# Linear attention's denominators gathered into one PSUM bank per superblock

## The chip, the cores and the metric

One core of one Trainium2 chip. The metric is device microseconds (us) of one execution: the kernel before has a median of 287.94 us over 3 runs (287.43 to 290.42). The profiled execution took 287.51 us, of which 285.5 us are its span from the first to the last instruction.

## The reference

Two attention blocks, A and B, run on inputs of their own (2048 tokens, width 640, 32 heads of 20), and their outputs stand side by side. A is a softmax with a sliding window of 256 tokens. B is linear attention, and the change is in B alone:

```python
def _B_ref(x, wqkv, wo):
    ...
    phi = lambda t: jnp.where(t > 0, t + 1, jnp.exp(t)) + 1e-6
    pq, pk = phi(q), phi(k)
    kv = jnp.einsum("bhsd,bhse->bhde", pk, v)
    z = jnp.einsum("bhsd->bhd", pk)
    num = jnp.einsum("bhqd,bhde->bhqe", pq, kv)
    den = jnp.einsum("bhqd,bhd->bhq", pq, z)[..., None] + 1e-6
    o = num / den
    return (lambda x, *d: x.transpose(*d))(o, 0, 2, 1, 3).reshape(B, S, D) @ wo
```

## The kernel before

The 2048 tokens are four superblocks of 512 (`SB`), each of four token blocks of 128 (`TPS`); the width of 640 is five chunks of 128 (`KT`). The main loop is written out by hand and goes through 90 **units** of A. A unit multiplies queries with keys into the four-bank tile `S_ps` on TensorE (PE), takes the exponential `p<-S_ps` on ScalarE (ACT), masks it on GpSimd (POOL), and two units later multiplies the result with the values into `O_ps` (PE, 16 short matmuls of 21 columns), which VectorE (DVE) divides into `otokA` (`recA`, then `otokA`). `S_ps` has one buffer, so the score matmuls of a unit start only when the exponential of the unit before has ended.

Everything else is **fill**: generators that yield how many matmul columns they have issued, and from which `take` pulls after each unit. The constants `EARLY`, `FILL` and `TAIL` fix how many columns are taken: (352320 - 17920 - 2 * 1024) / 90, about 3692 columns a unit. What the fill still has after the last unit is issued at once, and then comes `a_out_last`, the output projection of A's last superblock, which needs the transposes `oT<-otokA` that SP (SyncE) issues after the last `O_ps`.

Fill of block B that matters here:

- `b_q(s)` projects the queries of superblock s, one bank for each of the five chunks. `phi` takes the exponential on ACT at once (`e<-dense`), but its two DVE operations (`rest`: `e<-e`, then `phi<-dense,e`) are put into the list `later`. `flush()` records them behind the next evacuation or the next `phi`.
- `b_num(s)` makes numerators and denominators together. `kv_bd` holds for each head 20 columns of k-v sums and, as column 21 (`HV` = `DH` + 1), the sum of phi(k); heads that a chunk doesn't own are zero. For each of 4 token blocks and 2 halves of 16 heads, 3 matmuls (147, 147 and 84 columns) fill one bank, and DVE does `denB<-dense` (an add of 1e-6), `denB<-denB` (the reciprocal) and `otokB<-dense,denB` (the multiplication). Half 0 reads the chunks 0 to 2 of phi(q), half 1 the chunks 2 to 4. After each token block SP issues one transpose `xA<-otokB`.
- `outs` are the output projections, in the order `a_out(0)`, `b_out(0)`, ... `b_out(2)`, each of five banks: four of 5 matmuls of 512 columns and one of 20 matmuls of 128. `early` are A's projections for its last superblock.
- `even(a, na, b, nb, lead)` mixes banks of two generators; with `lead=True` a bank of `b` comes first.

All these banks come from the pool `dense` (`dps`), which has 3 buffers. A fourth bank can be filled only when the evacuation of the first is done. PE, DVE, ACT, POOL and SP each run their own instructions strictly in the order in which the program recorded them.

Of the kernel before, what the change touches and what calls it, by code (L numbers as in the profile page):

```python
# [9 lines left out]
P = 128  # L10
# [3 lines left out]
BF16 = mybir.dt.bfloat16  # L14
F32 = mybir.dt.float32

H = 32
DH = 20
HV = DH + 1
NG = H // 4  # L20
SB = 512
TPS = SB // P
# [32 lines left out]
def kernel(  # L55
# [10 lines left out]
    nc = tc.nc  # L66
    _, S, D = A_x.shape
    KT = D // P
# [8 lines left out]
    def pool(name, bufs, space=None):  # L77
        if space is None:
            return ctx.enter_context(tc.tile_pool(name=name, bufs=bufs))
        return ctx.enter_context(tc.tile_pool(name=name, bufs=bufs, space=space))  # L80
# [11 lines left out]
    rp = pool("rows", 4)  # L92
    op = pool("o", 2)
    sp = pool("small", 4)
    sps = pool("sps", 1, PSUM)
    ops = pool("ops", 1, PSUM)
    dps = pool("dps", 3, PSUM)
# [55 lines left out]
    heads_of = []  # L153
# [24 lines left out]
    def flush():  # L178

        while later:  # L180
            later.pop(0)()
# [8 lines left out]
    def bank():  # L190
        return dps.tile([P, SB], F32, name="dense")
# [9 lines left out]

    def phi(dst, src, view=lambda t: t[:]):

        e = sp.tile([P, SB], BF16, name="e")
        nc.scalar.activation(out=view(e), in_=src, func=ACT.Exp)  # L205
        flush()

        def rest():
            nc.vector.tensor_scalar(  # L209
                out=e[:], in0=e[:], scalar1=1e-6, scalar2=1.0 + 1e-6, op0=ALU.add, op1=ALU.min  # L210
            )
            nc.vector.scalar_tensor_tensor(  # L212
                out=dst, in0=src, scalar=0.0, in1=view(e), op0=ALU.max, op1=ALU.add
            )

        later.append(rest)
# [4 lines left out]
    def even(a, na, b, nb, lead=False):  # L221


        def one(g):
            for c in g:
                yield c
                if isinstance(c, End):
                    break

        done = 0  # L230
        for i in range(na):
            while lead and done < nb and done * na <= i * nb:
                done += 1
                yield from one(b)
            yield from one(a)
            while not lead and done * na < (i + 1) * nb:
                done += 1
                yield from one(b)
        yield from a


    xA, xB = {}, {}
# [18 lines left out]
    def a_qk(s, between=()):  # L261
        for n, base in (("q", 0), ("k", D)):
            st = stp.tile([P, KT, SB], BF16, name="st")
            for c in range(KT):
                ps = bank()
                yield from chain(
                    ps[:],
                    lambda kt: w_sb["A"][:, kt, base + c * P : base + (c + 1) * P],
                    lambda kt: xA[s][:, kt, :],
                    SB,  # L270
                )
                evac(st[:, c, :], ps[:])
                if c == KT - 1:
                    pad, pl, name = (q_pad, qp, "qpad") if n == "q" else (k_pad, kp, "kpad")
                    pad[s] = pl.tile([P, NG, SB], BF16, name=name)
                    if n == "q":
                        q_reads = bounce(n, s, st, pad[s])
                        for g in between:
                            yield from g
                    else:  # L280
                        late_reads[s] = bounce(n, s, st, pad[s])
                        q_reads()
                yield End(SB)
# [30 lines left out]
    def a_v(s):  # L314
        v_tok[s] = v_bufs[s % 3]
        yield from v_proj("A", xA[s], v_tok[s])
# [42 lines left out]
    kv_bd = wp.tile([P, KT, NHC, HV], BF16, name="kv_bd")  # L359

    def b_kv(s):
        pk = pqp.tile([P, TPS, D], BF16, name="phi")

        def done(tb, ps):
            if tb is None:
                phi(pk[:, :, SB:D], ps, lambda t: t[:].rearrange("p (t n) -> p t n", n=P))
            else:
                phi(pk[:, tb, 0:SB], ps[:])

        rows = tok_rows(xB[s], w_sb["B"], D, done)  # L370
        values_of = v_proj("B", xB[s], vB)
        yield from even(rows, TPS + 1, values_of, TPS + 1)
        yield from values_of
        flush()
# [22 lines left out]
    hh = H // 2  # L397
    half_parts = []
    for i in range(2):
        parts = []  # L400
        for c in range(KT):
            a, b = heads_of[c]
# [5 lines left out]
    oT_B = {}  # L408

    pq_of = {}  # L410

    def b_q(s):
        xt = xB[NS + s]
        pq = pqp.tile([P, KT, SB], BF16, name="phi")
        pq_of[s] = pq
        for c in range(KT):
            ps = bank()
            yield from chain(
                ps[:],
                lambda kt: w_sb["B"][:, kt, c * P : (c + 1) * P],  # L420
                lambda kt: xt[:, kt, :],
                SB,
            )
            phi(pq[:, c, :], ps[:])
            if s == 0:
                keep_own_head(kv_bd, c)
            yield End(SB)

    def b_num(s):
        flush()  # L430
        pq = pq_of[s]
        oT_B[s] = xp.tile([P, KT, SB], BF16, name="xA")
        for tb in range(TPS):
            ot = rp.tile([P, D], BF16, name="otokB")
            for i in range(2):
                ps = bank()
                ov = ps[:, 0 : hh * HV].rearrange("p (h e) -> p h e", e=HV)
                parts = half_parts[i]
                for n, (c, ho, nh, col) in enumerate(parts):
                    nc.tensor.matmul(  # L440
                        ov[:, col : col + nh, :],
                        lhsT=pq[:, c, tb * P : (tb + 1) * P],
                        rhs=kv_bd[:, c, ho : ho + nh, :],
                        start=(n == 0),
                        stop=(n == len(parts) - 1),
                        skip_group_check=True,
                    )
                den = sp.tile([P, hh, 1], F32, name="denB")
                nc.vector.tensor_scalar_add(
                    out=den[:], in0=ov[:, :, DH:HV], scalar1=1e-6  # L450
                )
                nc.vector.reciprocal(out=den[:], in_=den[:])
                nc.vector.tensor_tensor(  # L453
                    out=ot[:, i * hh * DH : (i + 1) * hh * DH].rearrange(
                        "p (h e) -> p h e", e=DH
                    ),
                    in0=ov[:, :, 0:DH],
                    in1=den[:].to_broadcast([P, hh, DH]),
                    op=ALU.mult,
                )  # L460
                flush()
                yield End(3 * 150)
            nc.sync.dma_start_transpose(
                out=oT_B[s][:, :, tb * P : (tb + 1) * P], in_=ot[:]
            )

    def b_out(s):
        yield from wo_proj("B", oT_B[s], s, D)
# [102 lines left out]
    def a_out(s):  # L571
        yield from wo_proj("A", oT_A[s], s, 0)
# [22 lines left out]
    def load(n, s):  # L595
        if n == "A":
            xA[s] = load_x("A", s)
        else:
            xB[s] = load_x("B", s % NS)
        yield 0  # L600

    def seq(*gens):
        for g in gens:
            yield from g
# [27 lines left out]
    def k_reads(s, gen):  # L632
        return hook(gen, 8, lambda: late_reads[s]())

    early = seq(a_v(3), a_qk(3))
    outs = seq(a_out(0), b_out(0), a_out(1), b_out(1), a_out(2), b_out(2))
# [13 lines left out]
        b_kv(3),  # L650
        load("B", NS + 1),
        even(b_q(0), KT, early, 2),
        load("B", NS + 2),
        even(b_num(0), 2 * TPS, early, 2 * TPS, lead=True),
        early,
        k_reads(3, b_q(1)),
        load("B", NS + 3),
        even(b_num(1), 2 * TPS, outs, 2 * TPS, lead=True),
        even(b_q(2), KT, outs, 2),
        even(b_num(2), 2 * TPS, outs, 2 * TPS, lead=True),  # L660
        even(b_q(3), KT, outs, 2),
        even(b_num(3), 2 * TPS, outs, 2 * TPS, lead=True),
        outs,
        b_out(3),
    )
# [16 lines left out]
    for i, (okey, first, last, parts) in enumerate(units):  # L682
        p = scores(okey[0], parts)
# [44 lines left out]
```

## Time and profile before

| | |
|---|---|
| median of 3 runs | 287.94 us |
| profiled execution: its time, its span | 287.51 us, 285.5 us |
| busy: PE, DVE, ACT, POOL | 271.2, 181.4, 199.5, 159.5 us |
| granted TensorE clock | 0.999 |
| `kv_bd` matmuls of `b_num` (L440) | 96 |
| `denB<-dense` (L449), `denB<-denB` (L452), `otokB` (L453) | 32 each; mean 164, 253, 492 ns |
| first and last of the L440 matmuls | 157.9 and 267.4 us |

Busy time of an engine is the time in which one of its recorded instructions ran. Matmuls overlap one another, so a duration of one (173 ns for 21 columns) says little of how fast a row of them is issued. In a line of the timeline stand start and duration in us, engine, line of the kernel, operation, output<-input, and how many; in square brackets how long the engine was idle before it and for whom it waited. ACT's exponential `p<-S_ps` marks the units: the time from the start of one to the start of the next is the length of a unit.

### The profile page before, as it was taken

The numbers are of one execution on the slowest core, as the hardware profiler recorded it, in microseconds if no ns is written. First come the engines' busy times: TensorE is split into PE (matmuls) and PEld (weight loads), VectorE is DVE, ScalarE is ACT, GpSimd is POOL, SyncE is SP. The second block draws the span as 40 slices with busy tenths as digits, with TensorE's granted clock in tenths as the row PEclk, the third lists the DMA queues.
The fourth block names the chain that finished last, engine by engine and source line by source line (L and its number), as shares of the span: only waits on it lengthen the run. The fifth ranks groups of instructions, "written<-read, shape, count | busy, mean of one in ns | idle before, by whom it ended". The sixth has DMA issues, their size and how long they took to land.

```text
span 285.5 us, 8251 instructions
## 1 busy us (share of the span) xinstructions
PE 271.2 (95%) x3512; PEld 156.7 (55%) x3512; DVE 181.4 (64%) x409; ACT 199.5 (70%) x227; POOL 159.5 (56%) x205
## 2 busy tenths in 40 slices
PE   7999999898999999999998799998999989999995
PEld 7644555564655754555654464444655555546652
DVE  0666657549656745547656785468866886678861
ACT  2000069968979888889889588897889868978402
POOL 4000036656656666666678666665766776676620
PEclk9999999999999999999999999999999999999999
DMA  7997699989152762273053522179865228022566
GB/s 247 296 316 217 165 206 178 109 162 270 32 117 47 146 88 94 72 144 63 3 117 72 115 49 77 40 171 125 148 137 72 79 61 141 3 78 64 136 172 200
DMA packets 68116, 35.91 MB, mean 126 GB/s; under 512 B 50800, under 2 KB 67184, under 8 KB 68080
## 3 DMA queue, kind: packets, MB, share of 16 engines
q1 hardware_dynamic: 65760, 29.50, 51.7%
q0 software_dynamic: 1008, 4.59, 4.7%
q10 hardware_dynamic: 1312, 1.31, 1.5%
q8 instruction: 27, 0.44, 0.7%
q14 instruction: 9, 0.07, 0.1%
HBM read 12.45 MB, written 10.49 MB: 80 GB/s over the span
## 4 chain that ended last, share of the span: by engine, by line
PE 81%; DVE 7%; ACT 5%; issue 5%; DMA 2%; POOL 0%; ACTq 0%; POOLq 0%
PE dense L196 53%; PE O_ps L533 14%; PE S_ps L489 10%; ACT p L497 3%; DMA oT<-otokA 2%; PE dense L148 1%; PE dense L440 1%; PE dense L381 1%; DVE osb L187 1%; ACT e L205 1%; DVE e L209 1%; DVE otokA L556 1%; DVE phi L212 1%; DVE vB L187 1%; DVE recA L555 1%
## 5 line engine op out<-in xcount | busy, mean ns | idle before, releaser
L511 POOL TENSOR_SCALAR_AFFINE_SELECT p<-p 128x512 bf16<-128x512 bf16 (+2 forms) x178 | 147.5, 829 | 110.6 <-ACT p L497 102.6
L497 ACT ACTIVATE p<-S_ps 128x2048 bf16<-128x2048 f32 x90 | 168.7, 1875 | 47.1 <-PE S_ps L489 46.7
L533 PEld LDWEIGHTS <-p 128*128 128x128 bf16 x1440 | 42.4, 96 | 20.1 <-issue 19.0
L533 PE MATMUL O_ps<-vA,p 128*128 128x21 bf16 x1440 | 50.9, 173 | 1.4 <-issue 1.4
L196 PE MATMUL dense<-wB,xB 128*128 128x320 bf16 (+2 forms) x320 | 49.0, 298 | 1.2 <-DVE phi L212 0.7
L196 PE MATMUL dense<-xA,wA 128*128 128x512 bf16 x200 | 46.2, 379 | 0.0
L187 DVE CAST st<-dense 128x512 bf16<-128x512 f32 x40 | 27.5, 690 | 20.3 <-PE dense L196 18.7
L489 PE MATMUL S_ps<-qpad,kpad 20*128 20x256 bf16 (+2 forms) x736 | 35.9, 269 | 1.0 <-ACT p L497 0.4
L187 DVE CAST osb<-dense 128x512 bf16<-128x512 f32 (+1 forms) x39 | 25.2, 647 | 15.1 <-PE dense L196 14.7
L196 PEld LDWEIGHTS <-xA 128*128 128x128 bf16 x320 | 26.2, 97 | 15.6 <-DVE otokB L453 1.4
L196 PEld LDWEIGHTS <-xB 128*128 128x128 bf16 x320 | 26.0, 97 | 12.9 <-issue 0.8
L489 PEld LDWEIGHTS <-kpad 20*128 20x128 bf16 x736 | 13.1, 92 | 31.9 <-issue 29.8
L196 PEld LDWEIGHTS <-wA 128*128 128x128 bf16 x200 | 18.5, 97 | 19.6
L212 DVE SCALAR_TENSOR_TENSOR phi<-dense,e 128x512 bf16<-128x512 f32 x40 | 27.7, 691 | 1.4
L482 ACT ACTIVATE p<-ident 1x1 bf16<-1x1 bf16 x90 | 17.0, 188 | 15.7 <-DVE st L187 15.4
L196 PE MATMUL dense<-woA,oT 128*128 128x512 bf16 (+1 forms) x160 | 25.9, 299 | 1.8 <-DVE osb L187 1.7
L196 PE MATMUL dense<-wA,xA 128*128 128x320 bf16 x160 | 25.2, 299 | 1.8 <-DVE otokB L453 1.0
L187 DVE CAST vB<-dense 128x320 bf16<-128x320 f32 x32 | 15.5, 490 | 17.1 <-PE dense L196 17.0
L196 PE MATMUL dense<-woB,xA 128*128 128x512 bf16 (+1 forms) x160 | 25.4, 299 | 0.7 <-DVE otokB L453 0.7
L196 PE MATMUL dense<-xB,wB 128*128 128x512 bf16 x100 | 25.0, 378 | 0.8 <-DVE phi L212 0.6
L209 DVE TENSOR_SCALAR e<-e 128x512 bf16<-128x512 bf16 x40 | 19.5, 487 | 9.2 <-ACT e L205 8.9
L205 ACT ACTIVATE e<-dense 128x512 bf16<-128x512 f32 x40 | 23.2, 592 | 1.2 <-PE dense L196 1.0
(33 smaller groups left out, 155.8 us busy)
## 6 DMA issues: line engine op xcount, KB each, us to landing
out_dram<-osb POOLq DMA_DIRECT2D x7, 640.0 KB, 4.1
qpad<-q_scr SPq DMA_DIRECT2D x16, 160.0 KB
kpad<-k_scr SPq DMA_DIRECT2D x16, 160.0 KB
wA<-in_A_wqkv_dram SPq DMA_DIRECT2D x3, 800.0 KB
wB<-in_B_wqkv_dram SPq DMA_DIRECT2D x3, 800.0 KB
q_scr<-st SPq DMA_DIRECT2D x3, 640.0 KB
k_scr<-st SPq DMA_DIRECT2D x3, 640.0 KB
woA<-in_A_wo_dram SPq DMA_DIRECT2D x1, 800.0 KB
```

Of the source, the lines that this page charges most:

```text
L148: nc.tensor.matmul(ps[:, 0:P], lhsT=ident[:], rhs=ident[:], start=True, stop=True)
L187: nc.vector.tensor_copy(out=dst, in_=src)
L196: nc.tensor.matmul(dst, lhsT=lhs(kt), rhs=rhs(kt), start=(kt == 0), stop=(kt == KT - 1))
L205: nc.scalar.activation(out=view(e), in_=src, func=ACT.Exp)
L209: nc.vector.tensor_scalar(out=e[:], in0=e[:], scalar1=1e-6, scalar2=1.0 + 1e-6, op0=ALU.add, op1=ALU.min)
L212: nc.vector.scalar_tensor_tensor(out=dst, in0=src, scalar=0.0, in1=view(e), op0=ALU.max, op1=ALU.add)
L381: nc.tensor.matmul(pv, lhsT=pk[:, tb, c * P : (c + 1) * P], rhs=vB[:, tb, a : b + 1, :], start=(tb == 0), stop=(tb == TPS - 1),)
L482: nc.scalar.activation(out=p_all[0:1, 4 * SB : 4 * SB + 1], in_=ident[0:1, 0:1], func=ACT.Copy)
L489: nc.tensor.matmul(S_ps[:, j, blk * P : blk * P + n], lhsT=kt[32 * j : 32 * j + DH, g, ko : ko + P], rhs=q_pad[s][32 * j : 32 * j + DH, g, ...
L497: nc.scalar.activation(out=p, in_=S_ps[:], func=ACT.Exp, scale=scale)
L511: nc.gpsimd.affine_select(out=v, in_=v, pattern=[[0, 4], [0, b1 - b0], [sgn, P]], compare_op=ALU.is_ge, fill=0.0, base=0 if kind == "D" el ...
L533: nc.tensor.matmul(O_ps[:, slot, j, :], lhsT=p[:, j, b * P : (b + 1) * P], rhs=v_tok[kb // TPS][:, kb % TPS, 4 * gg + j, :], start=(first ...
```

## The change

For each superblock a new generator `b_den` makes all denominators first: 20 matmuls (4 token blocks by 5 chunks) of 7 or 8 columns, whose moving operand is column 21 of `kv_bd`, into one bank as 4 x 32 columns. One add of 1e-6 and one reciprocal over 128 x 128 elements follow. `b_num` then multiplies numerators only (140, 140 and 80 columns), and DVE does one multiplication for each half. `divide` issues one bank of the partner generator, then `b_den`, then the mix of `b_num` with the partner as before, with 8, 8, 7 and 6 partner banks. `b_den` yields 20 * 64 = 1280 columns; a half still yields 450, and `EARLY`, `FILL` and `TAIL` stay. The tile `e` gets a pool of its own with 3 buffers instead of 4, `denB` one with 2.

```diff
+    ep = pool("e", 3)
+    dp = pool("den", 2)
...
-        e = sp.tile([P, SB], BF16, name="e")
+        e = ep.tile([P, SB], BF16, name="e")
...
+    def banks(g, n):
+
+        for _ in range(n):
+            for c in g:
+                yield c
+                if isinstance(c, End):
+                    break
+
+    def divide(s, g, n):
+
+
+        yield from banks(g, 1)
+        yield from b_den(s)
+        yield from even(b_num(s), 2 * TPS, g, n, lead=True)
...
+    def b_den(s):
+
+        flush()
+        ps = bank()
+        dv = ps[:, 0 : TPS * H].rearrange("p (t h) -> p t h", h=H)
+        for tb in range(TPS):
+            for c in range(KT):
+                a, b = heads_of[c]
+                nc.tensor.matmul(
+                    dv[:, tb, a : b + 1],
+                    lhsT=pq_of[s][:, c, tb * P : (tb + 1) * P],
+                    rhs=kv_bd[:, c, 0 : b - a + 1, DH],
+                    start=(tb == 0 and c == 0),
+                    stop=(tb == TPS - 1 and c == KT - 1),
+                    skip_group_check=True,
+                )
+        rden = dp.tile([P, TPS, H, 1], F32, name="denB")
+        rden_of[s] = rden
+        nc.vector.tensor_scalar_add(out=rden[:, :, :, 0], in0=dv, scalar1=1e-6)
+        nc.vector.reciprocal(out=rden[:], in_=rden[:])
+        yield End(TPS * KT * 64)
+
     def b_num(s):
-        flush()
...
-                ov = ps[:, 0 : hh * HV].rearrange("p (h e) -> p h e", e=HV)
+                ov = ps[:, 0 : hh * DH].rearrange("p (h e) -> p h e", e=DH)
...
-                        rhs=kv_bd[:, c, ho : ho + nh, :],
+                        rhs=kv_bd[:, c, ho : ho + nh, 0:DH],
...
-                den = sp.tile([P, hh, 1], F32, name="denB")
-                nc.vector.tensor_scalar_add(
-                    out=den[:], in0=ov[:, :, DH:HV], scalar1=1e-6
-                )
-                nc.vector.reciprocal(out=den[:], in_=den[:])
                 nc.vector.tensor_tensor(
...
-                    in0=ov[:, :, 0:DH],
-                    in1=den[:].to_broadcast([P, hh, DH]),
+                    in0=ov,
+                    in1=rden_of[s][:, tb, i * hh : (i + 1) * hh, :].to_broadcast([P, hh, DH]),
                     op=ALU.mult,
                 )
...
-        even(b_num(0), 2 * TPS, early, 2 * TPS, lead=True),
+        divide(0, early, 2 * TPS),
...
-        even(b_num(1), 2 * TPS, outs, 2 * TPS, lead=True),
+        divide(1, outs, 2 * TPS),
         even(b_q(2), KT, outs, 2),
-        even(b_num(2), 2 * TPS, outs, 2 * TPS, lead=True),
+        divide(2, outs, 7),
         even(b_q(3), KT, outs, 2),
-        even(b_num(3), 2 * TPS, outs, 2 * TPS, lead=True),
+        divide(3, outs, 6),
         outs,
         b_out(3),
```

More of the change, by code (lines that the diff above doesn't have):

```diff
@@ L427, in b_q @@
             yield End(SB)
+    rden_of = {}
+    def b_den(s):
[18 more added lines that the diff above has]
+        yield End(TPS * KT * 64)
     def b_num(s):
-        flush()
         pq = pq_of[s]
@@ L461, in b_num @@
                 flush()
+                if i == 1:
+                    nc.sync.dma_start_transpose(
+                        out=oT_B[s][:, :, tb * P : (tb + 1) * P], in_=ot[:]
+                    )
                 yield End(3 * 150)
-            nc.sync.dma_start_transpose(
-                out=oT_B[s][:, :, tb * P : (tb + 1) * P], in_=ot[:]
-            )
     def b_out(s):
```

## The prediction

> **What bounds the kernel now.** I read the page's busy times and its chain of waits first, then the timeline of single units, then the end of the span.
>
> ```profile
> PE 271.2 (95%) x3512; PEld 156.7 (55%) x3512; DVE 181.4 (64%) x409; ACT 199.5 (70%) x227; POOL 159.5 (56%) x205
> ...
> PE 81%; DVE 7%; ACT 5%; issue 5%; DMA 2%; POOL 0%; ACTq 0%; POOLq 0%
> ```
>
> DVE, from which the change takes work, is busy for 64% and holds 7% of the chain; so its busy time is worth nothing by itself, only where PE waits for it. Next, the timeline of an undisturbed unit:
>
> ```profile
> 237.86 1.88 ACT L497 ACTIVATE p<-S_ps 128x2048 bf16<-128x2048 f32 x1 [0.41 <-PE S_ps L489]
> ...
> 239.79 0.40 PE L489 MATMUL S_ps<-qpad,kpad 20*128 20x256 bf16 x8
> ...
> 240.12 0.56 PE L533 MATMUL O_ps<-vA,p 128*128 128x21 bf16 x16
> 240.23 1.88 ACT L497 ACTIVATE p<-S_ps 128x2048 bf16<-128x2048 f32 x1 [0.41 <-PE S_ps L489]
> ```
>
> A unit lasts 240.23 - 237.86 = 2.37 us: an exponential, then the scores, in turn. PE has in the same time 0.33 for the scores, 0.50 for the 16 O_ps matmuls (0.031 each in the chain, L533) and the fill, 7 matmuls of 512 columns in 1.52 (0.217 each). So ACT with the scores and PE are nearly level. A unit with 8 such matmuls takes 2.58; one in which ACT has two `e` between exponentials takes 2.82 (188.53 to 191.35).
>
> I add up the 42 units from the exponential that starts at 157.29 to the last, at 265.74, each at the larger of 2.37, its PE work, and 2.82 if it has two `e`: 102.8 us. The trace has 108.45. The 5.7 us between are waits in the four `b_num` stages, in units of 4.06, 3.04, 3.33, 2.63, 3.67 and 3.24 us above all. One of these, the first of superblock 3:
>
> ```profile
> 253.13 0.38 PE L196 MATMUL dense<-woA,oT 128*128 128x512 bf16 x1
> ...
> 253.34 0.33 PE L440 MATMUL dense<-kv_bd,phi 128*128 128x147 bf16 x3
> ...
> 253.54 0.69 DVE L187 CAST osb<-dense 128x512 bf16<-128x512 f32 x1 [1.74 <-PE dense L196]
> 254.15 0.28 DVE L209 TENSOR_SCALAR e<-e 128x512 bf16<-128x512 bf16 x1
> ...
> 254.28 1.24 PE L196 MATMUL dense<-woA,oT 128*128 128x512 bf16 x5 [0.62 <-DVE osb L187]
> ...
> 254.46 0.69 DVE L212 SCALAR_TENSOR_TENSOR phi<-dense,e 128x512 bf16<-128x512 f32 x1
> ```
>
> PE fills two banks and waits for the copy `osb` to free a third. What matters most for the forecast is DVE's order here: the partner's copy first, then `e<-e`, and only then the last chunk of phi(q), which ends at 255.15, 1.8 us after PE finished the partner bank (253.35). PE goes on at 254.28, since half 0 doesn't read that chunk.
>
> Last, the end:
>
> ```profile
> 270.58 0.55 PE L533 MATMUL O_ps<-vA,p 128*128 128x21 bf16 x16
> ...
> 270.98 5.38 PE L196 MATMUL dense<-woB,xA 128*128 128x512 bf16 x39
> ...
> 271.98 6.18 SPq L567 DMA_TRANSPOSE oT<-otokA  x4
> ...
> 276.42 5.61 PE L196 MATMUL dense<-woA,oT 128*128 128x512 bf16 x40
> ```
>
> The fill left behind the last unit (39 matmuls) ends at about 276.3, and the transposes let `a_out_last` go at 276.42. The two are level, so more fill here lengthens the end.
>
> **The change, part by part.**
>
> *DVE.* Removed per superblock: 8 x (164 + 253) ns = 3.3 us. Added: one add, 164 + 112 more elements at about 1 ns (128x240 to 128x320 takes 407 to 491 ns, L556), 0.28 us; and one reciprocal of 128 elements, which by 128x12 to 128x16 (230 to 254 ns, L555) takes 6 ns for each, 254 + 112 x 6 = 0.93 us; at 1 ns for each, the least in these rows, 0.37. DVE saves 2.1 us, 8.5 in all, off the path except at bank waits. The 0.93 us lie beside the partner bank (1.09 us of PE) and the unit's scores and O_ps (0.83); without that cover they would cost up to 0.3 us each.
>
> *Bank waits.* A pair of partner copy and half cost DVE 0.61 + 0.20 + 0.29 + 0.40 = 1.5 us from start to start, now 1.0, against 1.25 us of PE. So the second and later waits of a stage go: of the 5.7 us nothing of the old kind is left, except in superblock 2, where with 7 partner banks two halves come one after another and the next partner bank finds its copy unfinished, 0.4 us.
>
> *The new wait.* `b_den` reads all five chunks, and its fifth matmul is the first on the last chunk, whose phi is recorded behind the partner's copy. From the rows above: partner bank done, 0.19 to the copy's start, 0.61, 0.31, 0.69, 0.05 to PE = 1.85 us, less four den matmuls (0.12): PE waits 1.73 us. Behind it on PE stand the other den matmuls, the scores of the next unit (so ACT's exponential) and its O_ps. Superblock 0: the partner is a 320-column bank; before, it ended at 157.99 with the half behind it, and phi at 159.57, so 1.6. Superblock 1: 1.7, of which 0.5 is hidden, since the unit before has two `e` and ACT is late by itself; 1.2. Superblock 2: 1.65. Superblock 3: before the copy, DVE still has `recA`, `otokA` (0.70 together) and the fourth chunk's rest (0.92), so the copy starts 0.25 late: 1.9. With the 0.4 from above 6.75 us, against 5.7: **+1.05**. The phi itself may not be shortened by anything in the change.
>
> *PE work.* 20 den matmuls at 0.031 (the O_ps row, also one weight load and few columns each) are 0.62 us a superblock, against 8 x 16 columns saved, 0.05. Bounds: a gain is excluded, as 20 instructions are added; upward, a 128-column matmul takes 0.054 (20 in 1.09) and an unpipelined weight load 0.096 (PEld, L533), so 0 to 1.9 us a block; I take 0.62, the nearest row. Taking is by columns, so in the loop a block replaces 1280 columns (0.53) of other fill: adding up the new order in the same way gives 103.0 instead of 102.8, **+0.2**.
>
> [...]
>
> *The end.* `FILL` stays while 4 x 1280 columns come in, so the loop leaves as much more undone. In the new order 23 matmuls of 512 and 40 of 128 columns follow the last O_ps, instead of 19 and 20: 4 x 0.217 + 20 x 0.054 = +1.95. Shortly before it two halves meet again, and a partner bank waits 0.5 for its copy where before 0.24 were lost: **+2.2** in all. The transposes land well before PE now gets to them, so their 0.2 of idle time goes too, within the rounding. `xA<-otokB` keeps its place on SP ahead of `oT<-otokA`; its last one has 3 us to spare.
>
> *At nothing:* three `e` buffers (only 3 banks exist, so no fourth `e` is open), the pool of `denB` (a superblock apart).
>
> Sum on the profiled execution: 287.5 + 1.05 + 0.2 + 2.2 = **291.0 us**; on the median, 0.4 more.
>
> **Rivals.**
>
> *Faster:* the den matmuls don't wait, and the shorter hold of banks is what counts. Then 287.5 - 5.7 + 0.4 + 0.2 + 2.2 = 284.6. For it: in all of before PE waited 0.2 us for phi in front of a `kv_bd` matmul. Against: half 0 never asked for the last chunk, and in superblock 3 phi ends 1.8 us after the partner bank. The sign turns where the four waits fall below (5.7 - 0.4 - 2.4) / 4 = 0.7 us each. 0.08.
>
> *The end absorbs its fill:* SP's transposes come later than I think or PE gets through faster, so the 2.2 were waiting time: 288.8. For it, both ended together at 276.4; against, the 39 matmuls ran without a gap. 0.17.
>
> *Short matmuls are dear:* at 0.054 us, 80 x 0.023 = +1.8, 292.8; at 0.096, 296.2. For it, a strided moving operand that no row shows; against, the O_ps row. 0.10.
>
> *The forecast:* 0.65.
>
> **How the numbers follow.** The likeliest gives 291.0. The range takes in the second rival (288.8) and dear matmuls at 0.054 on top of the median's 0.4 (293.2): 288.6 to 293.2, leaving out the faster case and the 0.096. One per cent, 2.9 us, is about what a measurement here tells from no change; it ends at 290.4 on the profiled run, 290.8 on the median. Of the forecast's 0.65, whose waits may be off by 0.4 us each, I put 0.42 above that; with the dear matmuls slower is 0.52, faster (below 284.6 to 285.1) 0.07, the rest 0.41.
>
> **What would show it.** Right: in each superblock 4 den matmuls, then some 1.2 to 1.9 us of PE idle for DVE phi; four units of over 4 us; other units of the stages at 2.4 to 2.6; the reciprocal near 0.93 us; den matmuls 31 ns apart; about 63 matmuls after the last O_ps, and `a_out_last` without a wait for DMA. Wrong: den matmuls that start right behind the partner bank, or an end no longer than before's 14.5 us after the last O_ps.

## The result, and the profile after

The changed kernel takes a median of 300.22 us (296.28 to 300.75, 4 runs), beside 288.02 us (4 runs) for the kernel before: a ratio of 1.035 (1.028 to 1.043). It is slower, as forecast, but by far more than forecast, and outside the range of 288.6 to 293.2 us. Ratios, here and below, leave out executions more than 1.5% above the fastest of their kernel, so they are not the quotients of the medians.

The page of the profiled execution (296.28 us) first: busy times, the granted clock in 40 slices of 7.4 us, the chain that ended last.

```profile
span 294.6 us, 8343 instructions
...
PE 276.2 (94%) x3592; PEld 160.1 (54%) x3592; DVE 174.0 (59%) x353; ACT 199.4 (68%) x227; POOL 159.0 (54%) x205
...
PEclk9999999999999999999999999986999999997999
...
PE 74%; DVE 8%; DMA 6%; ACT 5%; issue 4%; SPq 0%; POOL 0%; ACTq 0%; POOLq 0%
```

DVE has lost 7.4 us of work, and nothing came of it. PE's busy time grew by 5.0 us. The line to stop at is the clock: before, all 40 digits were 9; here three are 8, 6 and 7. Then what PE waited for (engine, line and tile, releaser: total us, times, longest):

```profile
PE dense L456 <- DVE phi L214: 7.1, 5, 1.8
...
PE dense L198 <- DMA oT<-otokA: 0.7, 1, 0.7
```

The den matmuls (L456) do wait for phi, 7.1 us in all. The timeline of the den block of superblock 1 shows both the wait and what follows it:

```profile
194.62 0.26 PE L456 MATMUL dense<-kv_bd,phi 128*128 128x7 bf16 x4
...
194.96 0.68 DVE L189 CAST osb<-dense 128x512 bf16<-128x512 f32 x1
...
195.56 0.28 DVE L211 TENSOR_SCALAR e<-e 128x512 bf16<-128x512 bf16 x1
...
195.88 0.69 DVE L214 SCALAR_TENSOR_TENSOR phi<-dense,e 128x512 bf16<-128x512 f32 x1
...
196.62 0.59 PE L456 MATMUL dense<-kv_bd,phi 128*128 128x7 bf16 x16 [1.75 <-DVE phi L214]
...
198.14 2.29 PE L198 MATMUL dense<-woA,oT 128*128 128x512 bf16 x5
```

Four den matmuls, then copy, `e<-e` and phi on DVE, 1.75 us of idle PE, and the other 16: this is the order that the forecast drew. But the next 5 matmuls of 512 columns take 2.29 us, and such a row took 1.24 us before. A table of stretches (length; busy us of PE, PEld, DVE, ACT, POOL with counts; granted clock; DMA share; GB/s) shows why, in the stages of superblocks 1, 2 and 3:

```profile
193.00:210.00 17.00, 15.25 (x225) 8.50 (x218) 10.15 (x20) 10.93 (x14) 8.93 (x11) 0.80 0.81 94
226.00:243.00 17.00, 14.90 (x237) 8.74 (x240) 10.75 (x22) 12.71 (x16) 10.71 (x14) 1.00 0.22 60
256.00:273.00 17.00, 14.71 (x221) 8.57 (x218) 10.78 (x21) 11.81 (x13) 10.41 (x14) 0.90 0.16 50
```

0.80 over 17 us is (1 - 0.80) x 2 x 17 = 6.8 us on half the clock, 0.90 is 3.4 us. In finer stretches the clock is 0.5 for 6.83 us from 196.50, that is from the last 0.12 us of this wait, and for 3.41 us from 264.77, 2.2 us behind the two waits of superblock 3. So two things have to be kept apart: what the waits take themselves, and the half clock that the work behind them ran on.

### The profile page after: what moved, and what is told of

Its sections match the earlier page's. It is cut to its first block, busy times and chain, and to the rows that moved or that the text cites. A ratio compares the mean times of both kernels' runs of the same rounds, so it can differ in the third digit from the quotient of the medians.

```text
span 294.6 us, 8343 instructions
## 1 busy us (share of the span) xinstructions
PE 276.2 (94%) x3592; PEld 160.1 (54%) x3592; DVE 174.0 (59%) x353; ACT 199.4 (68%) x227; POOL 159.0 (54%) x205
## 4 chain that ended last, share of the span: by engine, by line
PE 74%; DVE 8%; DMA 6%; ACT 5%; issue 4%; SPq 0%; POOL 0%; ACTq 0%; POOLq 0%
PE dense L198 46%; PE O_ps L569 13%; PE S_ps L525 10%; ACT p L533 3%; DMA k_scr<-st 2%; DMA oT<-otokA 2%; DVE phi L214 2%; DMA kpad<-k_scr 2%; DVE e L211 2%; DVE osb L189 2%; PE dense L480 2%; PE dense L150 1%; ACT e L207 1%; PE dense L398 1%; DVE otokA L592 1%
## 5 line engine op out<-in xcount | busy, mean ns | idle before, releaser
L189 DVE CAST st<-dense 128x512 bf16<-128x512 f32 x40 | 27.4, 690 | 21.2 <-PE dense L198 20.8
L525 PE MATMUL S_ps<-qpad,kpad 20*128 20x256 bf16 (+2 forms) x736 | 36.7, 274 | 1.3 <-ACT p L533 0.6
L198 PE MATMUL dense<-woA,oT 128*128 128x512 bf16 (+1 forms) x160 | 28.2, 319 | 1.1 <-DMA oT<-otokA 0.7
```

The source lines that it names most:

```text
L189: nc.vector.tensor_copy(out=dst, in_=src)
L198: nc.tensor.matmul(dst, lhsT=lhs(kt), rhs=rhs(kt), start=(kt == 0), stop=(kt == KT - 1))
L525: nc.tensor.matmul(S_ps[:, j, blk * P : blk * P + n], lhsT=kt[32 * j : 32 * j + DH, g, ko : ko + P], rhs=q_pad[s][32 * j : 32 * j + DH, g, ...
```

## The experiments

The theory was: the den matmuls wait for phi, and the gaps on PE halve its granted clock for 3.41 us or twice that. Its rivals: the waits cost their own length and the rest is work at the end; or the den matmuls themselves are slow. All ratios are to the kernel before, run beside each. That kernel had medians of 289.5 to 290.1 us in these comparisons: it is not always on the whole clock either (287.1 to 290.0 us in runs with a mean clock of 0.997 or more, 290.1 to 291.2 in most of those at 0.992 to 0.994).

**PE kept busy during the wait.** In the changed kernel 8 matmuls of 384 columns are added ahead of the den matmuls; they write columns of the bank that nothing reads.

```diff
         dv = ps[:, 0 : TPS * H].rearrange("p (t h) -> p t h", h=H)
+        for _ in range(8):
+            nc.tensor.matmul(
+                ps[:, TPS * H : SB], lhsT=ident[:], rhs=wo_sb["A"][:, 0, 0 : SB - TPS * H],
+                start=True, stop=True, skip_group_check=True,
+            )
```

> The changed kernel with 8 matmuls of 384 columns more in front of each den block, written into columns of its bank that nothing reads: about 1.3 us of TensorE work inside a wait of 1.4 to 2.3 us, and nothing else is moved. Theory 1 (a gap of TensorE halves its clock): the waits for phi stay where they are, the clock stays at 1.0, and the time is the forecast's sum with 0.7 more for a wait at the end: 291 to 293 us, although work was added. Theory 2 (waits and work cost their own length): 300 us or up to 5 us more. Theory 3 (slow den matmuls): 300 us or more.

Measured: 293.36 us (292.80 to 296.24), ratio 1.019 (1.010 to 1.027). With 32 more matmuls the kernel is faster than without them, by 1.7% in the ratios, whose intervals don't touch, and 6.9 us in the medians; its four executions all lie below the seven of the changed kernel on record here (296.28 to 302.73 us). The same stage and the same stretches:

```profile
194.48 1.46 PE L454 MATMUL dense<-woA,ident 128*128 128x384 bf16 x8
...
195.74 0.69 DVE L214 SCALAR_TENSOR_TENSOR phi<-dense,e 128x512 bf16<-128x512 f32 x1
195.78 0.25 PE L461 MATMUL dense<-kv_bd,phi 128*128 128x7 bf16 x4
...
196.49 0.58 PE L461 MATMUL dense<-kv_bd,phi 128*128 128x7 bf16 x16 [0.46 <-DVE phi L214]
...
197.75 1.24 PE L198 MATMUL dense<-woA,oT 128*128 128x512 bf16 x5
```

```profile
193.00:210.00 17.00, 16.47 (x262) 10.19 (x259) 11.83 (x24) 12.88 (x16) 11.14 (x15) 1.00 0.78 108
226.00:243.00 17.00, 16.21 (x249) 9.58 (x251) 11.37 (x23) 12.17 (x14) 10.71 (x14) 1.00 0.26 63
256.00:273.00 17.00, 15.29 (x223) 9.49 (x220) 11.98 (x23) 10.00 (x10) 10.11 (x13) 1.00 0.35 103
```

The 16 den matmuls start just as late behind phi (0.06 us after it ends, there 0.05), but PE was idle for 0.46 us instead of 1.75; the clock stays at 1.00, and the row of 5 takes 1.24 us again. The late phi is the same in both kernels; only the idle PE differs.

**Half as many of them** (4 instead of 8).

```diff
-        for _ in range(8):
+        for _ in range(4):
```

> The changed kernel with 4 instead of 8 matmuls of 384 columns in front of each den block: 0.64 us of TensorE work in each wait, so that gaps of about 0.9, 1.1, 1.0 and 1.4 us are left, where the changed kernel has 1.4 to 1.8 us (and 2.3 in superblock 3) and the run with 8 has 0.5 to 0.6. Theory 1, with the dose that the runs so far show: between the two, about 294 us (293 to 298), with one or two halvings of the clock in most runs. If only gaps over some length between 1.3 and 1.4 us halved the clock: 292 to 293 us as with 8. Theories 2 and 3: 298 us or more.

Measured: 295.62 us (293.68 to 296.59), ratio 1.020 (1.014 to 1.026). Its waits:

```profile
PE dense L461 <- DVE phi L214: 3.7, 4, 1.1
```

In its profiled run (294.80 us) all stages are on the whole clock and the 42 units of the loop (those that the forecast added up) take 111.18 us, as with 8 (111.19). The one halved stretch lies at 59.2 to 62.6 us, outside of the stages, behind a gap that has nothing to do with the change. The same place before, and in this run:

```profile
57.01 0.20 PE L533 MATMUL O_ps<-vA,p 128*128 128x21 bf16 x2 [1.42 <-issue]
```

```profile
57.87 0.20 PE L574 MATMUL O_ps<-vA,p 128*128 128x21 bf16 x2 [2.39 <-issue]
```

Here PE stops ahead of the last two of 16 `O_ps` matmuls, for nothing that the profile shows ("issue"): in nine profiles of the case, for 0.9 us (the profile of the result) to 3.5 us (half 1 first in the kernel before, below). So gaps of up to 1.1 us in the stages left the clock alone in this run; its other runs, at 0.987 to 0.994, have no profile.

**The changed kernel again, unedited**, twice.

> The changed kernel once more, unedited, since its usual run of 300 us has no profile yet (the profiled one took 296.28 us with 10.24 us on half the clock). Theory 1 (waits that halve the granted clock): a run of about 300 us shows a mean clock of 0.971 to 0.976, that is 2 x 0.024 to 0.029 x 298 = 14 to 17 us, four or five stretches of 3.41 us, on half the clock, all of them behind PE's waits for phi in the four stages; units on the whole clock are as long as with the 8 extra matmuls. Theory 2 (the rest lies elsewhere): still about 10 us on half the clock, and the remaining 4 us in other units, in transfers or in the end.

> The same kernel a second time, to see whether the clock is halved in the same stages. Theory 1: halved behind the waits of at least two of the four superblocks, not necessarily the same ones; time = 293 us and some 1 to 2 us for each 3.41 us at half. Theory 2: no relation of time and stretches at half clock.

Measured: 296.63 us (profiled) and 302.73 in the first, 296.81 (profiled) in the second. The same stretches in the first:

```profile
193.00:210.00 17.00, 14.89 (x221) 8.52 (x223) 10.79 (x22) 12.10 (x15) 9.54 (x12) 0.90 0.85 106
226.00:243.00 17.00, 15.01 (x225) 8.57 (x227) 10.09 (x20) 11.79 (x15) 9.74 (x13) 0.90 0.21 60
256.00:273.00 17.00, 13.98 (x224) 8.48 (x226) 11.92 (x21) 12.36 (x15) 10.65 (x14) 1.00 0.17 50
```

and in the second:

```profile
193.00:210.00 17.00, 15.05 (x233) 9.00 (x235) 11.12 (x23) 13.28 (x16) 10.68 (x14) 1.00 0.87 111
226.00:243.00 17.00, 14.83 (x220) 8.56 (x221) 10.85 (x21) 11.41 (x14) 9.85 (x13) 0.90 0.18 49
256.00:273.00 17.00, 14.28 (x196) 8.12 (x198) 10.30 (x20) 10.73 (x13) 9.33 (x13) 0.80 0.16 50
```

Three executions of one kernel, with the same waits (7.1 us, longest 1.8, in all three), and the clock is halved in superblocks 1 and 3, in 1 and 2, in 2 and 3. That separates cause from coincidence unit by unit (counted from 0; us from one exponential's start to the next):

| units | stage | profile of the result | again, first | again, second | with 8 extra matmuls |
|---|---|---|---|---|---|
| 61 to 63 | superblock 1 | 11.01 (6.83 us halved) | 9.84 (3.41 halved) | 8.64 | 8.65 |
| 74 to 76 | superblock 2 | 9.71 | 10.68 (3.41 halved) | 10.64 (3.41 halved) | 9.71 |
| 85 to 87 | superblock 3 | 10.96 (3.41 halved) | 10.00 | 12.04 (6.83 halved) | 10.00 |

Where the clock is whole, the stage is as long as with the extra matmuls, to 0.01 us; each 3.41 us at half costs 0.9 to 1.2 us. Taking the shortest of the three for each of the 42 units gives 111.06 us for the loop, against 114.51, 113.34 and 114.15 measured. The first theory's wider claim, a usual run's 14 to 17 us at half clock all in the stages, got no test: no execution of 300 us was profiled. Those ran at a mean clock of 0.971 to 0.976, and the one of 302.73 at 0.966.

The traces also show where the clock changed. In the profile of the result the stretches between changes last 6.83, 61.44, 3.41 and 27.31 us, that is 2, 18, 1 and 8 times 3.413. In "again, first" it fell at 198.22 and 232.36 and rose at 201.64, 30.7 us or 9 times 3.413 before the second fall; in "again, second" it fell at 231.24 and rose 3.40 us later. So the changes lie on a grid of 3.41 us in these profiles, and the waits lie on it at another place in each: the one of superblock 1 ends 0.12 us behind a tick in the first and 0.51 us behind one in the last (197.62, the tick at 197.11). That this is why one program comes out differently each time is the author's estimate. The windows of the profile of the result between two ticks, with the waits in superblocks 1, 2 (two windows) and 3:

```profile
193.09:196.50 3.41, 1.78 (x29) 1.06 (x25) 3.14 (x7) 2.54 (x5) 2.33 (x4) 1.00 1.66 141
227.22:230.64 3.42, 2.45 (x35) 1.20 (x33) 2.73 (x7) 3.42 (x4) 2.28 (x3) 1.00 0.41 148
230.64:234.05 3.41, 2.76 (x51) 1.72 (x52) 2.05 (x4) 1.15 (x3) 1.78 (x2) 1.00 0.03 5
261.36:264.77 3.41, 2.17 (x45) 1.46 (x46) 2.40 (x5) 1.21 (x1) 0.31 (x1) 1.00 0.02 5
```

Length less busy PE is its idle time: 1.63 us in the first and 1.24 in the last, and both are followed by half the clock; the wait in superblock 2 is split by a tick into windows with 0.97 and 0.65 us, and the clock stays. No other window of that profile, from 25 us to the last matmul, holds more than 1.04 us. The four falls of the two repeats come behind windows with 1.6 to 2.1 us. But a window with 1.28 us (superblock 0 of "again, first", 157.26 to 160.67) was followed by the whole clock, and so was one with 1.24 (superblock 1 of "again, second", 193.69 to 197.11), as much as was followed by half of it above. So the idle time of a window doesn't decide alone.

**phi ahead of the partner's copy.** In the changed kernel the last chunk's rest is recorded first.

```diff
     def divide(s, g, n):
 
 
+        flush()
         yield from banks(g, 1)
```

> The changed kernel, but the last chunk's phi is recorded ahead of the partner bank's copy, so that VectorE makes it first. Theory 1 (the den matmuls wait for that phi, and these gaps of TensorE halve its granted clock for 3.4 or 6.8 us at a time): the gap in front of the fifth den matmul falls from 1.4-2.3 us to about 1.5 in superblock 0 (there GpSimd's last mask of kv_bd ends at 159.5 anyway), 0.6, 0.4 and 1.3 us; the clock stays at 1.0 or is halved once; 288.5 to 291 us. Theory 2 (the waits cost their own length and no more; the rest of the loss is work added at the end and elsewhere): 300.2 - 2.8 = about 297 us. Theory 3 (the den matmuls themselves are what is slow): no change, 296 to 300 us.

Measured: 293.69 us (290.43 to 297.50), ratio 1.013 (1.003 to 1.022). The page's clock and two of the waits of its profiled run (294.76 us):

```profile
PEclk9999999999999999999999799997999999999999
```

```profile
PE dense L457 <- DVE phi L214: 3.2, 4, 1.2
...
PE dense L457 <- POOL kv_bd L167: 1.3, 1, 1.3
```

The waits for phi fall from 7.1 to 3.2 us, so the partner's copy ahead of phi was half of them; one for `kv_bd`, in superblock 0, was under them. Yet the clock is halved for 3.41 us in superblocks 0 and 1, behind gaps no longer than 1.3 us. One run, at 0.999, took 290.43 us. The median is neither the theory's 288.5 to 291 us nor its rival's 297: the waits are shorter, but the clock was halved more often than forecast.

**The wait without den matmuls.** In the kernel before, half 1, which reads the last chunk, goes first.

```diff
-            for i in range(2):
+            for i in (1, 0):
```

> The kernel before, with the two halves of each token block in exchanged order, so that the half which reads the last chunk of phi comes first: the change's wait without any of its arithmetic. Theory 1: gaps of 1.6 to 2 us in front of the first half of each superblock; 287.9 + 3.4 = 291.3 us where the clock stays whole, and 2 to 8 us more where it is halved: 291 to 299 us, with a granted clock below 0.99 in the trace. Theory 2: 291.3 us with a clock of 0.999. Theory 3: 287.9 us, as no den matmul is in it.

Measured: 294.59 us (292.27 to 297.22), ratio 1.017 (1.007 to 1.027). An exchange of two halves, with no instruction added, costs about as much as the changed kernel with its PE kept busy. Its run at a mean clock of 0.998 took 292.27 us, some 4 us above before's; here 1.4 us of before's waits for `otokB` remain beside 6.1 us of waits for phi. Its profiled run (297.22 us, its longest) is on half the clock for 3.41 us behind two of these waits, of 1.64 and 1.40 us in superblocks 1 and 2, in a kernel that has no den matmuls, and a third time at 58.7 us, where the gap outside of the stages is 3.5 us long.

**phi first in the kernel before** (`flush()` ahead of the mix in all four stages):

```diff
+    def phi_first(a, na, b, nb, lead=False):
+
+        flush()
+        yield from even(a, na, b, nb, lead)
...
-        even(b_num(0), 2 * TPS, early, 2 * TPS, lead=True),
+        phi_first(b_num(0), 2 * TPS, early, 2 * TPS, lead=True),
```

> The kernel before, with the last chunk's phi recorded ahead of the partner bank's copy in each b_num stage: it tells how much of a gain of the first run comes from that order alone, without the merged denominators. The bank waits of the second and later halves stay, as VectorE still does an add, a reciprocal and a multiplication for each half: 287.9 us, within 1 us on either side, with a clock of 0.999, by all theories.

Measured: 287.73 us (10 runs), ratio 0.997 (0.992 to 1.002): no difference that this shows. Before, half 0 covered the late phi.

**The den block after two or three partner banks, phi first.** This takes the new wait away and leaves the gathered denominators.

```diff
-    def divide(s, g, n):
+    def divide(s, g, n, ahead):
 
-
-        yield from banks(g, 1)
+        flush()
+        yield from banks(g, ahead)
...
-        divide(0, early, 2 * TPS),
+        divide(0, early, 6, 3),
...
-        divide(1, outs, 2 * TPS),
+        divide(1, outs, 7, 2),
...
-        divide(2, outs, 7),
+        divide(2, outs, 6, 2),
...
-        divide(3, outs, 6),
+        divide(3, outs, 5, 2),
```

> The changed kernel with the last chunk's phi first, and the den block two partner banks later (three in superblock 0, where a mask of GpSimd comes late), the partner banks in all as many as before. Theory 1: no gap of TensorE over 0.6 us in the four stages, so the clock stays whole; the loop takes 103 us where it took 108.45 plus some 1.5 us of waits where two halves meet, and the end 3.1 us more (22.9 against 19.8 us, from the second run): 287.5 - 3.9 + 3.1 = 286.7 us, 285.5 to 288. Theory 2 (work at the end and elsewhere): 295 us or more. Theory 3 (slow den matmuls): 295 us or more.

Measured: 290.66 us (12 runs), ratio 1.004 (1.000 to 1.009). PE no longer waits for phi at the den block, and the clock is 1.0 in the profiled run (289.29 us). The loop takes 106.04 us, 2.4 less than before; the end, from the last exponential's start, takes 23.0 instead of 19.8. So the change's own gain exists, 2.4 us of the loop (2.2 beside phi first alone, whose loop takes 108.24), and is smaller than what it adds to the end. The 285.5 to 288 us forecast for this run were too few: the loop was expected at about 104.5 us, and 7 of the 12 executions have a mean clock of 0.994 or less, although these waits are gone.

**The same with `FILL` at 357440**, which takes 5120 more columns inside the loop, the 4 x 1280 that `b_den` added.

```diff
-FILL = 352320
+FILL = 357440
```

> The same with FILL raised by the 4 * 1280 columns that the den blocks yield, so that the loop takes them and not the end. Adding up the units gives 1.9 us more in the loop (18 more units with eight matmuls, or other work over 2.37 us), and the end is 2.0 us shorter by its matmuls and 0.9 more by its wait for a transpose, if that wait goes: 0 to 1 us less than the run before it, 285.5 to 287 us, by theory 1. By theory 2 (the end is what is lost) 3 us less.

Measured: 291.03 us (12 runs), ratio 1.004 (0.999 to 1.008). The loop takes 106.25 us and the end 21.2, with a new wait of 1.6 us for the last transposes; the median doesn't follow, and 285.5 to 287 us had been forecast. Nothing is won.

**Extra matmuls in the kernel before**: 8 of 176 columns ahead of the first half of each superblock, to see whether its own runs at 0.992 to 0.994 come from the stages.

```diff
                 parts = half_parts[i]
+                for _ in range(8 if tb == 0 and i == 0 else 0):
+                    nc.tensor.matmul(
+                        ps[:, hh * HV : SB], lhsT=ident[:], rhs=wo_sb["A"][:, 0, hh * HV : SB],
+                        start=True, stop=True, skip_group_check=True,
+                    )
```

> The kernel before with 8 matmuls of 176 columns (0.6 us) put ahead of the first half of each superblock, into columns of its bank that nothing reads. Theory 1, extended (the runs of the kernel before that take 290 us and more have a granted clock of 0.994 or less, so its own waits of 0.4 to 0.7 us a piece already halve the clock now and then): the granted clock is 0.998 or more in nearly all runs, the median 287.5 to 289 us, and its spread smaller. If these runs have another cause: the same spread as the kernel before, with 0 to 2 us more for the added work.

Measured: 290.26 us (12 runs), ratio 1.003 (0.999 to 1.008), 5 of the 12 at 0.994 or less, beside 12 of 29 for the kernel before. That is the same share: these matmuls don't keep the runs on the whole clock, so it is not, or not only, the waits filled here that cost before its clock.

**phi first, and the reciprocal straight from the bank.** In the kernel before the add of 1e-6 to the denominators is left out, besides the edit of phi first.

```diff
-                nc.vector.tensor_scalar_add(
-                    out=den[:], in0=ov[:, :, DH:HV], scalar1=1e-6
-                )
-                nc.vector.reciprocal(out=den[:], in_=den[:])
+                nc.vector.reciprocal(out=den[:], in_=ov[:, :, DH:HV])
```

> The kernel before with the last chunk's phi first, and with the reciprocal taken straight from the bank: the addition of 1e-6 to the denominators is left out. The halves stay as they were and no den matmul is added, but VectorE does one operation less for each of the 32 halves, 0.20 us from start to start. Where TensorE waits for a bank (units of 3.0 to 3.7 us in the run with phi first) 0.2 to 0.4 us go each time, about 2 us in all, and with shorter gaps the clock is halved less often: span 283.5 to 285 us and 285.5 to 287 us on a whole clock, 0.985 to 1.0 of the kernel before by theory 1. By theory 2 the same gain from the waits alone, with no fewer halvings.

Measured: 287.66 us (285.87 to 290.07, 12 runs), ratio 0.995 (0.991 to 1.000), the lowest median of all, 0.07 us below phi first alone. Six runs are on the whole clock, at 285.87 to 287.38 us, about as forecast; but six are not, beside 10 of 17 for the kernel before, so fewer halvings don't show. Its loop takes 107.54 us. What was worth having in the change, a bank held for less time, comes here without a wait and without more work on PE, though also without the reference's 1e-6; with an interval that ends at 0.9995 and phi first alone at 0.997, the gain is small and its size uncertain.

## Why the prediction was wrong

The direction and the mechanism were right, and most terms were near:

- **The new wait.** PE was idle for phi for 1.42, 1.75 and 1.62 us in superblocks 0 to 2, against 1.6, 1.7 and 1.65 forecast. In superblock 3 the forecast had 1.9; there are two, of 0.79 and 1.49, because the den matmuls' bank is the one that the fourth chunk's phi must first free: 2.28 us in all, 0.4 more than forecast.
- **The den matmuls** came 27 ns apart (16 in 0.43 us, from 159.55 to 159.98 below), forecast 31. The rival of dear matmuls, at 54 or 96 ns, falls.

```profile
159.55 0.58 PE L456 MATMUL dense<-kv_bd,phi 128*128 128x7 bf16 x16 [1.42 <-DVE phi L214]
...
159.98 0.84 PE L198 MATMUL dense<-wA,xA 128*128 128x320 bf16 x5
```

- **DVE.** The by-shape groups have both operations as estimated, 0.93 and 0.28 us (in all DVE saved 7.4 us instead of 8.5, off the path):

```profile
L467 DVE RECIPROCAL denB<-denB 128x128 f32<-128x128 f32 x4 | 3.8, 953 | 0.1
...
L466 DVE TENSOR_SCALAR denB<-dense 128x128 f32<-128x128 f32 x4 | 1.2, 292 | 2.7 <-PE dense L456 2.7
```

- **The reciprocal's cover** failed in superblock 0: PE waits 0.25 us for an `otokB` behind it, and unit 49 takes 2.67 instead of 2.37. That is the 0.3 named for it.
- **The loop** on the whole clock takes 111.06 us, forecast 108.45 + 1.05 + 0.2 = 109.7. Of the 1.4 us too little, superblock 3 has 0.4 and the reciprocal 0.3; the rest isn't assigned unit by unit (units 75 and 76, where two halves meet, take 2.86 and 2.63).
- **The end** takes 22.8 us from the last exponential's start, before 19.8: 3.0 more, forecast 2.2. The 63 matmuls after the last `O_ps` are there, as counted, but the transposes did not land "well before PE now gets to them":

```profile
277.43 7.36 PE L198 MATMUL dense<-woB,xA 128*128 128x512 bf16 x63
...
279.04 6.65 SPq L603 DMA_TRANSPOSE oT<-otokA  x4
...
280.38 0.77 POOL L372 DMA_DIRECT2D out_dram<-osb  x1 [4.77 <-DVE osb L189]
...
284.62 1.52 PE L198 MATMUL dense<-woA,oT 128*128 128x512 bf16 x10
...
286.82 4.25 PE L198 MATMUL dense<-woA,oT 128*128 128x512 bf16 x30 [0.68 <-DMA oT<-otokA]
```

The first 10 matmuls of `a_out_last` start at once; the other 30 wait 0.68 us for the second transpose, whose data came 7.78 us after the first was issued (286.82 - 279.04). Before, where all 40 ran without a gap, it was there after at most 5.84 us (276.42 + 5.61 / 4 - 271.98). An output transfer of 640 KB starts at 280.38, in the midst of the transposes; before, one started at 271.55, 0.43 us ahead of them. That the later one holds them up is only argued.

All this together is 292.95 us, the profiled run with extra matmuls, or by the shortest units 296.28 - (114.51 - 111.06) = 292.8: inside the range. **The step that failed** is the price of the wait: the forecast took 1.6 to 1.9 us of idle PE at its own length, on a granted clock of 0.999 that it read from the profile of before and carried over. Before, no window of 3.41 us in the stages held more than 0.9 us of idle PE, and its clock stayed whole there. Behind the new waits the clock was 0.5 for 3.41 or 6.83 us, in two of the four stages in each of three profiles, and the loop took 2.3 to 3.5 us more (113.34 to 114.51, against 111.06). The usual run of 300.2 us has 0.971 to 0.976 instead of 0.983 and lost 4 us more; in which units, no profile shows. At 0.9 to 1.2 us for each 3.41 us, its 14 to 17 us on half the clock instead of 10.24 are worth 1.1 to 2.5 us (an estimate), so some 1.5 us or more of these 4 have no price yet. With the waits filled no run took more than 296.24 us, which suggests that they go with the waits too; the gap at 56 us, whose unit took 3.5 us in the profile of the result and up to 7.4 in another kernel's, could also have a part.

The rival of a faster kernel needed waits of less than 0.7 us: they were twice that. Its gain is real, as the experiment with the later den block shows, but only without the wait. That the end would absorb its fill fell too.

## What to carry to other kernels

The granted clock of 0.999 in the profile of before didn't hold once the change had opened gaps of 1.42 to 1.75 us on PE: in superblock 1 it was 0.80 over 17 us, and 1.00 when matmuls filled the same gap to 0.46. So a forecast for a change that opens such a gap should price the clock as well as the gap: here each 3.41 us at half cost 0.9 to 1.2 us. And it needs a spread from run to run, as the same wait was followed by 0, 3.41 and 6.83 us of it in three profiles. Before a small operation is gathered into an earlier one, look at which of its inputs is made last: here it was the last chunk of phi, which the old order of halves covered and one gathered block could not. A few matmuls into unused columns told here, in one run, that the wait cost the clock and not only its own length (ratio 1.019 against 1.035).

## What the hardware showed that was not expected

- The gap of 1.75 us on PE in superblock 1 was followed by 0, 3.41 or 6.83 us on half the clock in three executions of one program, and gaps of at most 1.3 us by 3.41 us twice in one run, with phi first; gaps of at most 1.1 us left the stages at 1.00 in another, with 4 extra matmuls. In the three profiles of the changed kernel the clock changed on a grid of 3.41 us, and a window with 1.24 us of idle PE was followed by half the clock in one and by the whole clock in another. What decides isn't settled.
- 32 useless matmuls lengthened the loop by 0.1 us (111.19 against 111.06 on the whole clock) and made the kernel faster, from a ratio of 1.035 to one of 1.019.
- The kernel before has a mean clock of 0.994 or less in 33 of the 62 executions run beside the experiments, and takes some 2 us or more longer in them. Its profile is of the whole clock, so the place isn't known. A candidate is PE's gap at 56 us, which needs no wait of the stages: where it was 2.39 us long (4 extra matmuls) and 3.5 (half 1 first), the profiles have 3.41 us of half the clock behind it; where it was 2.4 (the changed kernel with phi first), there is none.
